# Windowed attention beside a gMLP: one fixed order from attention through its output projection, seven exponential buffers, two maxima banks

## The chip, the cores and the metric

The kernel runs on one core of a Trainium2 chip. A core has five engines that work side by side and meet at semaphores: TensorE (PE, matmuls into PSUM, with its weight loads shown apart as PEld), VectorE (DVE), ScalarE (ACT), GpSimd (POOL) and SyncE (SP), which here issues all DMA transfers. Every engine takes its instructions in the order in which they stand in its own queue. The metric is the device time of one execution in microseconds, taken as the median of several runs.

## What is computed

```python
def _A_ref(x, wqkv, wo):                      # H = 32 heads of 18, window 256
    q, k, v = ...                             # x @ wqkv
    scores = einsum("bhqd,bhkd->bhqk", q, k) * (Dh ** -0.5)
    mask = (q_idx - k_idx >= 0) & (q_idx - k_idx < W)
    p = softmax(where(mask, scores, -1e9))
    return (p @ v) @ wo

def _B_ref(x, w_in, w_sp, b_sp, w_out):       # S = 2048, D = 576, Fh = 2304
    z = gelu(x @ w_in)
    z1, z2 = z[..., :Fh], layernorm(z[..., Fh:])
    g = einsum("ts,bsf->btf", w_sp, z2) + b_sp[None, :, None]
    return (z1 * g) @ w_out

xn = layernorm(x)
out = x + _A_ref(xn, wqkv, wo) * silu(_B_ref(xn, w_in, w_sp, b_sp, w_out))
```

## The kernel before

All large products run in a 32-bit format on TensorE that keeps only the upper part of a number, so each operand is split into a high part (an ACT copy) and a low part (a subtraction on DVE or POOL), and three products are added: high by high, high by low, low by high. The stages follow each other: layer norm and the projections to q, k, v and z2 (up to about 425 us of the trace); then **the attention, with the z1 projection as filler**; then **the output projection of the attention** (its matmuls are named wops); then the spatial product with w_sp (acc, from about 945 us) and the last product with w_out.

The attention works in 16 units of four heads and 1024 queries (`UNITS`, `NU`). The q and k of a unit are read from DRAM into slots (tiles `att`, line 550). For each unit:

- *Maxima* (`max_item`, tile `sp`): a matmul of 128 queries with up to 384 keys, then on DVE an addition of the band mask (`band`) with the row maximum (line 606). When all 32 of a unit are done, `max_split` puts the negative maxima into the tile `ms`, two transposes on TensorE and two DVE copies bring them into `mhl` (`max_turn`), and a DMA moves them as two extra rows beside q (line 637), so that the next matmul subtracts them.
- *Scores* (`scores`, tile `tps`, line 741): a matmul over a block of 128 keys, the exponential on ACT into the tile `pt` (line 745), masking of the two edge blocks on POOL (lines 753 and 756). One `pt` tile holds four heads of one key block.
- *Value products* (`pv`, tile `ops`, line 769): four heads in four column groups of TensorE; the column of ones in the values gives the sum of the exponentials. A step takes one `pt` tile: four matmuls.
- *End of a unit* (`finish`): the sums go through DRAM (`den`, `r_d`) and come back, inverted, as a broadcast tile `rp` (line 814); POOL multiplies (line 818, four divisions to a unit) and SP stores the result to `o_d` (line 823).

Maxima, scores and the matmuls of z1 use 64 of TensorE's 128 rows each: heads of even number and the bank `ma` the upper half, heads of odd number and `mb` the lower half, so two of them run at a time. Value products and wops use all rows.

The z1 projection (`z1_rows`, line 685) has 18 chunks of 128 features; for each half of the rows and each of two spans of 512 tokens, 27 matmuls (`STEPS`) add up in one bank. The weights of a chunk come by DMA into `z1raw`, and are split by ACT into `z1wh` and by POOL into `z1wl` (line 702). A finished bank is copied by ACT to `z1o` (line 690) and stored (line 573).

**What sets the order.** Within a region opened by `tc.manual_schedule` the instructions of the named engines stay in the order in which the code emits them. In the attention the code picks that order itself: a loop keeps an estimated clock for each half of the rows (`row_time`) and for ACT, DVE and POOL (`busy`), and at each step emits, on the half that is free first: a run of value products if `pv_now` allows it, else a transpose of maxima, else a score or a maximum that its estimate says can go, else one filler matmul of z1. A score needs a free score bank (`done_exp`), a free `pt` buffer (`PTB` of them) and moved maxima; a maximum needs a free bank among `SPB` (`done_max`). A run of value products starts when enough `pt` tiles are ready: nine blocks of 128 queries, or all `PTB` tiles in use. Transfers are put into the same order by estimated due times (`after`). Score and maxima banks share five banks of PSUM (`5 - SPB` and `SPB`).

Attention and projection stand in two such regions, one behind the other, and instructions of the second may be placed among the last of the first.

In the projection, `wo_split` rounds the attention output of 256 tokens (tile `ohl`: ACT line 1175, DVE line 1176, from a load at lines 999 and 1001), and `wo_half` multiplies 128 tokens with wo (line 1189, 28 matmuls); there are 16 of these half tiles. The ninth is the first that needs the result of the last unit.

## Time and profile before

| | us |
|---|---|
| three runs | 1841.81, 1843.65, 1845.96 |
| median | 1843.65 |
| the profiled execution, whole | 1847.18 |
| its span in the trace | 1845.3 |
| busy in the span: PE / PEld | 1822.1 / 1597.3 |
| busy in the span: DVE / ACT / POOL | 1133.8 / 945.1 / 430.4 |
| first score matmul (tps) starts | 442.18 |
| first matmul of the spatial product (acc) starts | 944.65 |

The profile lists busy time by engine, groups of instructions by line with the mean duration of one and the idle time ahead of them (and who ended it), waits, and a timeline. A matmul's duration is its way through the array, and several are under way at a time; what one costs is read from the distance between starts. "Granted clock" (PEclk) is TensorE's clock as a share of full speed. In a row of the timeline, x8 means eight records of that kind in succession.

### The profile page before, as it was taken

The numbers are of one execution on the slowest core, as the hardware profiler recorded it, in microseconds if no ns is written. First come the engines' busy times: TensorE is split into PE (matmuls) and PEld (weight loads), VectorE is DVE, ScalarE is ACT, GpSimd is POOL, SyncE is SP. The second block draws the span as 40 slices with busy tenths as digits, with TensorE's granted clock in tenths as the row PEclk, the third lists the DMA queues.
The fourth block names the chain that finished last, engine by engine and source line by source line (L and its number), as shares of the span: only waits on it lengthen the run. The fifth ranks groups of instructions, "written<-read, shape, count | busy, mean of one in ns | idle before, by whom it ended". The sixth has DMA issues, their size and how long they took to land.

```text
span 1845.3 us, 37698 instructions
## 1 busy us (share of the span) xinstructions
PE 1822.1 (99%) x14373; PEld 1597.3 (87%) x14373; DVE 1133.8 (61%) x2299; ACT 945.1 (51%) x1757; POOL 430.4 (23%) x509
## 2 busy tenths in 40 slices
PE   8999999999999999999999999999999999999998
PEld 8999999998778777877888888888888888899998
DVE  7321333468777776631156788667886576767876
ACT  5433322225777667774467566465554544544443
POOL 3332333435566456554000000111100000000000
PEclk9999999999999999999999999999999999999999
DMA  8895688888677867645776777789776556796554
GB/s 275 189 234 166 233 279 280 289 265 234 160 194 189 206 176 199 179 140 150 224 244 223 242 239 247 256 291 302 253 256 235 189 188 208 229 269 208 160 162 135
DMA packets 266916, 405.72 MB, mean 220 GB/s; under 512 B 52336, under 2 KB 180592, under 8 KB 266608
## 3 DMA queue, kind: packets, MB, share of 16 engines
q1 hardware_dynamic: 266736, 403.32, 72.0%
q8 instruction: 113, 1.85, 0.4%
q14 instruction: 67, 0.55, 0.1%
HBM read 285.35 MB, written 117.09 MB: 218 GB/s over the span
## 4 chain that ended last, share of the span: by engine, by line
PE 85%; DMA 5%; DVE 5%; ACT 2%; SPq 1%; issue 1%; POOL 0%; DVEq 0%; ACTq 0%; POOLq 0%
PE acc L1470 34%; PE mb L207 11%; PE c L1562 8%; PE ma L685 6%; PE mb L685 6%; PE ma L207 5%; PE ops L769 4%; PE tps L741 3%; PE wops L1189 3%; PE sp L603 3%; DMA st_d<-qkhl 1%; SPq L364 1%; PE mb L381 1%; DMA att<-st_d 1%; DVE spl L117 1%
## 5 line engine op out<-in xcount | busy, mean ns | idle before, releaser
L1470 PE MATMUL acc<-spl,zh 128*128 128x512 f32 x1008 | 392.6, 389 | 0.9 <-DVE spl L117 0.6
L1470 PE MATMUL acc<-sph,zh 128*128 128x512 f32 x1008 | 392.3, 389 | 1.1 <-ACT so L1222 1.1
L1470 PE MATMUL acc<-sph,zl 128*128 128x512 f32 x1008 | 392.2, 389 | 0.0
L606 DVE CUSTOM_DVE_ANT_0 sp<-sp,band 128x384 f32<-128x384 f32 (+1 forms) x512 | 265.0, 566 | 77.4 <-PE sp L603 43.4
L745 ACT ACTIVATE pt<-tps 128x384 f32<-128x384 f32 (+2 forms) x576 | 229.0, 441 | 99.6 <-PE tps L741 74.9
L117 DVE TENSOR_TENSOR spl<-spr,sph 128x1024 fp32r<-128x1024 f32 x168 | 210.2, 1251 | 43.8 <-ACT sph L116 42.8
L685 PE MATMUL mb<-b,z1wh 64*128 64x512 f32 x648 | 225.6, 399 | 0.1
L1470 PEld LDWEIGHTS acc<-spl,zh 128*128 128x128 f32 x1008 | 189.2, 188 | 41.8 <-DVE spl L117 2.6
L1470 PEld LDWEIGHTS acc<-sph,zh 128*128 128x128 f32 x1008 | 189.2, 188 | 40.8 <-ACT so L1222 1.5
L685 PE MATMUL ma<-b,z1wh 64*128 64x512 f32 x648 | 222.8, 401 | 0.4 <-ACT zt L968 0.4
L1470 PEld LDWEIGHTS acc<-sph,zl 128*128 128x128 f32 x1008 | 189.2, 188 | 39.1
L116 ACT ACTIVATE zh<-b 128x384 fp32r<-128x384 f32 x168 | 87.4, 520 | 208.1 <-PE acc L1470 208.0
L116 ACT ACTIVATE sph<-spr 128x1024 fp32r<-128x1024 f32 x168 | 176.0, 1047 | 17.6 <-DMA spr<-in_w_sp_dram 9.2
L117 DVE TENSOR_TENSOR zl<-b,zh 128x384 fp32r<-128x384 f32 x168 | 98.5, 586 | 123.2 <-ACT zh L116 117.8
L741 PE MATMUL tps<-att 56*128 56x384 f32 (+1 forms) x576 | 171.7, 343 | 2.4 <-DMA att<-mhl 1.8
L603 PE MATMUL sp<-att 54*128 54x384 f32 (+1 forms) x512 | 159.5, 349 | 1.3 <-DMA att<-st_d 0.9
L1562 PE MATMUL c<-b,o 128*128 128x288 f32 x1056 | 143.8, 295 | 1.9 <-DVE o L117 1.4
L1562 PEld LDWEIGHTS c<-b,o 128*128 128x128 f32 x1056 | 141.0, 188 | 2.6 <-DVE o L117 1.9
L969 DVE BATCH_NORM_STATS2 st<-zt 128x6 f32<-128x384 f32 x96 | 49.3, 549 | 131.5 <-ACT zt L968 131.3
L685 PE MATMUL ma<-b,z1wl 64*128 64x512 f32 x324 | 128.5, 397 | 0.0
L685 PE MATMUL mb<-b,z1wl 64*128 64x512 f32 x324 | 127.9, 395 | 0.0
L685 PEld LDWEIGHTS mb<-b,z1wh 64*128 64x128 f32 x648 | 117.9, 186 | 6.4 <-ACT z1o L690 1.5
(224 smaller groups left out, 4203.0 us busy)
## 6 DMA issues: line engine op xcount, KB each, us to landing
spr<-sc_d SPq DMA_DIRECT2D x96, 512.0 KB
spr<-in_w_sp_dram SPq DMA_DIRECT2D x72, 512.0 KB
zr<-z_d SPq DMA_DIRECT2D x144, 192.0 KB
z_d<-zt SPq DMA_DIRECT2D x48, 384.0 KB
z_d<-z1o SPq DMA_DIRECT2D x72, 256.0 KB
z1t<-z_d SPq DMA_DIRECT2D x72, 256.0 KB
y_d<-z1t SPq DMA_DIRECT2D x72, 256.0 KB
a<-in_w_sp_dram SPq DMA_DIRECT2D x64, 256.0 KB
```

Source lines behind the costliest of these rows:

```text
L116: act.activation(hi, src, AF.Copy)
L117: dve.tensor_tensor(lo, src, f32(hi), ALU.subtract)
L207: pe.matmul(banks[h][:, :n], *both[h][i], start=i == 0, stop=i == STEPS - 1)
L603: pe.matmul(ps[:, :w], q_of(u, j)[0:54, i * P:(i + 1) * P], k_of(u, j)[0:54, k0:k0 + w], start=True, stop=True)
L606: dve.tensor_tensor_reduce(out=ps[:, :w], in0=ps[:, :w], in1=band[:, m0:m0 + w], scale=1.0, scalar=-3.0e38, op0=ALU.add, op1=ALU.max, accu ...
L685: pe.matmul(ps, w, x_, start=n == 0, stop=n == STEPS - 1)
L741: pe.matmul(ps[:, :m * P], k_of(u, j)[:, (kb - base) * P:(kb - base + 1) * P], q_of(u, j)[:, (a - lo) * P:(a - lo + m) * P], start=True, s ...
L745: act.activation(pt[:, j, d0:d0 + n * P], ps[:, (qa - a) * P:(qa - a + n) * P], AF.Exp, scale=scale)
L769: pe.matmul(o_ps[c][32 * j:32 * j + 32, (qa - 4 * c) * P:(hi - 4 * c + 1) * P], vgs[u][:, kb - k0, j * VW:j * VW + 32], pt[:, j, (qa - kb) ...
L1189: pe.matmul(po[:, i, :288], lt[:, cs], r[:, i * 288:(i + 1) * 288], start=n == 0, stop=n == len(pl) - 1)
L1470: pe.matmul(acc[j], z[:, ps], w[:, cs], start=s == i == 0 and n in OPENS, stop=s == 7 and i == 2, skip_group_check=True)
L1562: pe.matmul(banks[key][:, :288], y, w, start=begin and k == n == 0, stop=close and k == 8 and n == 2, skip_group_check=True)
```

## The change

- Two banks for maxima in place of three (`SPB`), and so three for scores in place of two; seven `pt` buffers in place of five (`PTB`).
- Room for them: `z1raw` has one buffer in place of two and is loaded with its chunk (no load one chunk ahead, `fetch_z1` goes); `rp`, `mhl` and `ms` have one buffer in place of two; `band` is 384 wide in place of 512. The tile `rp` is taken only when its load is emitted, after the divisions of the unit before.
- The maxima of the first two query blocks are reduced over the columns that can count (128 and 256 in place of 256), and the estimate for DVE becomes 132 + w ns in place of 600 or 470.
- A run of value products waits for twelve blocks in place of nine (or all `pt` buffers).
- If a score and a maximum can both go on a half, the maximum goes first; before, the one whose engine had been done sooner.
- Attention and projection are one region of fixed order.

```diff
-SPB = 3
-PTB = 5
+SPB = 2
+PTB = 7
...
-    band = const.tile([P, 512], F32, name="band")
+    band = const.tile([P, 384], F32, name="band")
     pool.memset(band, 0.0)
-    pool.memset(band[:, 384:512], NEG)
...
-            halved = [aa.tile([P, P], F32R, name=f"ms{i}", bufs=1) for i in range(2)]
-            for ms in halved:
-                pool.memset(f32(ms), 0.0)
+            halved = aa.tile([P, P], F32R, name="ms", bufs=1)
+            pool.memset(f32(halved), 0.0)
...
-                dve.tensor_tensor_reduce(out=ps[:, :w], in0=ps[:, :w], in1=band[:, m0:m0 + w], scale=1.0,
+                w = 384 - m0
+                dve.tensor_tensor_reduce(out=ps[:, :w], in0=ps[:, :w], in1=band[:, m0:384], scale=1.0,
...
-                done_max.append(use("dve", 600 if w > 256 else 470))
+                done_max.append(use("dve", 132 + w))
...
-                    turned[u] = aa.tile([64, P], F32, name="mhl")
+                    turned[u] = aa.tile([64, P], F32, name="mhl", bufs=1)
...
-            def fetch_z1(f):
-                if f < FH // P and f not in z1raws:
-                    z1raws[f] = zw.tile([P, 9, P], F32, name="z1raw", bufs=2)
-                    sp.dma_start(z1raws[f], w_z1[f])
-
             def load_z1(f):
-                fetch_z1(f)
-                raw = z1raws[f]
-                wh = zw.tile([P, 9, P], F32R, name="z1wh")
-                wl = zw.tile([P, 9, P], F32R, name="z1wl")
+                raw = zw.tile([P, 9, P], F32, name="z1raw", bufs=1)
+                sp.dma_start(raw, w_z1[f])
+                wh, wl = (zw.tile([P, 9, P], F32R, name=n) for n in ("z1wh", "z1wl"))
...
-                                if b == 1 and n == 20:
-                                    fetch_z1(f + 2)
...
-                while len(parts.get(u - 2, ())) > 4:
-                    part(u - 2)
                 den = aa.tile([P, HS // 32], F32, name="den")
-                rp = ap_.tile([P, HS], F32, name="rp", bufs=2) if u < NU - 1 else f32(slots[4][:, 0:HS])
+                at = []
+
+                def rp():
+                    if not at:
+                        while len(parts.get(u - 1, ())) > 4 and u < NU - 1:
+                            part(u - 1)
+                        at.append(ap_.tile([P, HS], F32, name="rp", bufs=1) if u < NU - 1 else
+                                  f32(slots[4][:, 0:HS]))
+                    return at[0]
...
-                heads.enter_context(tc.manual_schedule(engines=ENGINES | {ET.Activation, ET.SP}))
+                order.enter_context(tc.manual_schedule(engines=ENGINES | {ET.Activation, ET.SP}))
...
-                        return n if size >= 9 or len(pts) >= PTB or not score_queue[0] else 0
+                        return n if size >= 12 or len(pts) >= PTB or not score_queue[0] else 0
...
-                        ready.append((done_exp[-1], 0))
+                        ready.append(0)
...
-                        ready.append((done_max[-1], 1))
+                        ready.append(1)
...
-                    if min(ready)[1]:
+                    if ready[-1]:
...
-            order.enter_context(tc.manual_schedule(engines=ENGINES | {ET.Activation, ET.SP}))
```

What this does to the order of instructions is seen in the queues. First TensorE in an early unit, around one run of value products; L603 and L741 are maxima and scores, L685 is z1, L769 the value products. Before:

```order
L685 MATMUL ma<-b_96,z1wh 128x512
L685 MATMUL mb<-b_97,z1wh 128x512
L769 MATMUL ops<-pt,vg 32x128 x4
L769 MATMUL ops<-pt,vg 32x256 x4
L769 MATMUL ops<-pt,vg 32x384 x4
L741 MATMUL tps<-att_6807 128x256
L603 MATMUL sp<-att_2213 128x384
```

and TensorE in the change, at a run near the same place (the lines are now L676, L758, L601 and L730):

```order
L676 MATMUL ma<-b_96,z1wh 128x512
L676 MATMUL mb<-b_92,z1wl 128x512
L758 MATMUL ops<-pt,vg 32x128 x4
L758 MATMUL ops<-pt,vg 32x256 x4
L758 MATMUL ops<-pt,vg 32x384 x8
L758 MATMUL ops<-pt,vg 32x256 x4
L758 MATMUL ops<-pt,vg 32x128 x4
L601 MATMUL sp<-att_2214 128x384 x2
L730 MATMUL tps<-att_2212 128x384 x2
```

The run holds six steps where it held three, and two maxima follow it ahead of the scores. Over the whole attention there were 68 runs (47 of three steps, 11 of one, 8 of two, 2 of four) and there are now 44 (14 of six, 2 of five, 12 of four, 5 of three, 8 of two, 3 of one).

Next TensorE at the seam between z1 (L685, now L676) and the projection (L1189, now L1183). Before, the first wops of all stand here, with z1 behind them again:

```order
L685 MATMUL mb<-b_96,z1wh 128x512
L1189 MATMUL wops<-att_2215,ohl_14367 128x288 x2
L1189 MATMUL wops<-att_6807,ohl_14367 128x288 x2
L1189 MATMUL wops<-att_2215,ohl_14367 128x288 x4
L1189 MATMUL wops<-att_6807,ohl_14367 128x288 x2
L1189 MATMUL wops<-att_2215,ohl_14367 128x288 x4
L1189 MATMUL wops<-att_6807,ohl_14367 128x288 x2
L685 MATMUL ma<-b_92,z1wh 128x512
```

and in the change, TensorE's last matmuls of z1 with the first wops behind them:

```order
L676 MATMUL mb<-b_93,z1wh 128x512
L676 MATMUL mb<-b_96,z1wh 128x512
L676 MATMUL mb<-b_93,z1wl 128x512
L1183 MATMUL wops<-att_2214,ohl_14361 128x288 x2
L1183 MATMUL wops<-att_6802,ohl_14361 128x288 x2
L1183 MATMUL wops<-att_2214,ohl_14361 128x288 x4
```

Before, 56 wops stood in four bursts among the last z1 matmuls; now none does.

Last, SP's queue of transfers at the same seam: z1 stores (L573 and L1153, now L572 and L1148), loads of attention output for the projection (L999 and L1001, now L994 and L996), the last unit's sums (den) and z2 for the spatial product (zr). Before:

```order
L830 DMA den<-att_13723 128x1x32
L150 DMA zr<-z_d 128x384 x4
L573 DMA z_d<-z1o 128x2x256
L828 DMA r_d<-den 128x32
L999 DMA att_13723<-o_d 128x4x256
L1001 DMA att_13723<-o_d 64x256 x2
L150 DMA zr<-z_d 128x384 x2
L573 DMA z_d<-z1o 128x2x256 x5
L999 DMA att_2213<-o_d 128x4x256
L1001 DMA att_2213<-o_d 64x256 x2
```

and SP in the change, where z1raw (L646) is the load of the last chunk of z1's weights:

```order
L572 DMA z_d<-z1o 128x2x256 x3
L646 DMA z1raw<-in_w_z_dram 128x1152
L572 DMA z_d<-z1o 128x2x256 x7
L994 DMA att_2212<-o_d 128x4x256
L996 DMA att_2212<-o_d 64x256 x2
L994 DMA att_2213<-o_d 128x4x256
L996 DMA att_2213<-o_d 64x256 x2
L1148 DMA z_d<-z1o 128x2x256 x2
L826 DMA den<-att_13613 128x1x32
L149 DMA zr<-z_d 128x384 x4
L824 DMA r_d<-den 128x32
```

The last unit's sums and the first loads of z2 stood among the z1 stores and now stand behind all of them; the load of the second 256 tokens stood behind the fifth of five stores, with one more store to come, and now has two stores behind it.

10 lines of the change are left out of this document (4 added, 6 removed).

## The prediction

> **What bounds the kernel now.** I read the busy time by stretch first, because the page's shares are averages over stages with different limits.
>
> ```profile
> core 0: us, PE busy (x) PEld busy (x) DVE busy (x) ACT busy (x) POOL busy (x), PEclk, DMA share, GB/s
> 431.00:857.00 426.00, 422.30 (x4260) 330.58 (x4256) 282.55 (x1044) 294.15 (x732) 240.21 (x352) 1.00 0.71 182
> 857.00:887.00 30.00, 29.68 (x198) 24.13 (x197) 0.90 (x3) 3.12 (x6) 0.00 (x0) 1.00 0.37 115
> 887.00:945.00 58.00, 54.63 (x394) 54.31 (x395) 15.24 (x19) 30.40 (x43) 2.54 (x2) 0.94 0.74 242
> ```
>
> The change acts on the first two stretches (attention with the z1 projection as filler, then the rest of that filler) and on where the third begins. In the first, TensorE is busy 422.3 of 426.0 us; DVE 282.6, ACT 294.2 and POOL 240.2 have room. So almost no waiting is left to remove here, and a shorter order of TensorE's own work is what can pay. Who TensorE waited for, between 430 and 890 us, says the same:
>
> ```profile
> engine line waited for: us in total, times, longest us
> PE tps L741 <- DMA att<-mhl: 1.8, 1, 1.8
> PE sp L603 <- DMA att<-st_d: 0.9, 1, 0.9
> ```
>
> The filler ends with the largest gap of the region, seen in TensorE's timeline:
>
> ```profile
> 886.39 0.39 PE L685 MATMUL ma<-b,z1wl 64*128 64x512 f32 x1
> 890.37 6.92 PE L1189 MATMUL wops<-att,ohl 128*128 128x288 f32 x33 [3.59 <-ACT ohl L1175]
> ```
>
> 3.59 us idle, until ACT has rounded the next 256 tokens of the attention output. That came late because SP stood in its queue behind five stores of z1:
>
> ```profile
> 862.23 21.81 SPq L573 DMA_DIRECT2D z_d<-z1o  x5
> 884.13 0.42 SPq L999 DMA_DIRECT2D att<-o_d  x1
> ```
>
> **Term 1: fewer switches into the value products.** A busy TensorE is not an efficient one. Maxima, scores and z1 use half the rows each and run in pairs; the value products (ops) use all rows, so before and behind each run of them both halves must drain and refill. TensorE's timeline at the end of the attention prices it:
>
> ```profile
> 846.65 0.39 PE L685 MATMUL mb<-b,z1wh 64*128 64x512 f32 x1
> 846.65 0.39 PE L685 MATMUL ma<-b,z1wl 64*128 64x512 f32 x1
> 846.97 1.50 PE L769 MATMUL ops<-pt,vg 128*32 128x128 f32 x24
> 848.41 0.49 PE L685 MATMUL ma<-b,z1wh 64*128 64x512 f32 x1
> 848.74 0.40 PE L685 MATMUL ma<-b,z1wh 64*128 64x512 f32 x1
> ...
> 852.04 0.50 PE L685 MATMUL ma<-b,z1wl 64*128 64x512 f32 x1
> 852.47 0.43 PE L769 MATMUL ops<-pt,vg 128*32 128x128 f32 x8
> 852.82 0.50 PE L685 MATMUL ma<-b,z1wh 64*128 64x512 f32 x1
> 853.16 0.40 PE L685 MATMUL ma<-b,z1wh 64*128 64x512 f32 x1
> 853.40 0.39 PE L685 MATMUL ma<-b,z1wl 64*128 64x512 f32 x1
> 853.63 0.40 PE L685 MATMUL ma<-b,z1wh 64*128 64x512 f32 x1
> ```
>
> Undisturbed, pairs start every 0.233 us (853.16, 853.40, 853.63). A matmul of ops leaves two records, and four heads make one step, so x8 is one step (here one block of 128 queries) and x24 three steps (1 + 2 + 3 = 6 blocks, by the shapes in the order). The short run: from 852.04 to 853.16 pass 1.12 us, less two pair steps of 0.233, leaves 0.65 us for one block. The long run: 846.65 to 848.74 is 2.09, less 0.47, leaves 1.62 us for six. So a block costs (1.62 - 0.65) / 5 = 0.19 us and a run, before its first block, 0.65 - 0.19 = 0.46 us. Both runs have 512-column z1 pairs beside them; many others have scores or maxima of 384 columns, whose half drains sooner, so I take 0.40 us. The order of before has 68 runs (47 of them of three steps), that of the change 44 (14 of six, 12 of four). 24 x 0.40 = **9.6 us saved**; ends: 0.30 each (7.2) and 0.46 each (11.0). The number of blocks, of maxima, of scores and of z1 matmuls is the same in both orders.
>
> **Term 2: the projection no longer starts inside z1.** Before, 56 wops matmuls stand in four bursts among the last z1 pairs; now all 448 follow the last z1 matmul. Their own time only moves. The four bursts go, each a drain and refill like a run of ops: 4 x 0.40 = **1.6 us saved**, ends 0 and 3, as each burst also left one half to run alone for some steps, which may or may not come back elsewhere.
>
> **Term 3: the gap at the seam.** The first wops now waits for the last z1 matmul, then for ACT: the last copy of z1 stands ahead of the rounding in ACT's order, and a DVE subtraction follows.
>
> ```profile
> 883.06 0.60 ACT L690 ACTIVATE z1o<-mb 128x512 f32<-128x512 f32 x1 [2.89 <-PE mb L685]
> 889.04 1.27 ACT L1175 ACTIVATE ohl<-att 128x1280 fp32r<-128x1280 f32 x1 [1.58 <-DMA att<-o_d]
> 855.58 1.55 DVE L1176 TENSOR_TENSOR ohl<-att,ohl 128x1024 fp32r<-128x1024 f32 x1 [10.95 <-ACT ohl L1175]
> ```
>
> 0.60 + 1.27 = 1.9 us until the first four products, which need the high part alone; then about 0.7 more until the low part: those four take about 0.5 of the subtraction's 1.2 to 1.55. About 2.6 us in place of 3.59, so **1.0 us saved**; ends 0 and 3.6. The load of the next tokens (L999) now stands ahead of the last two z1 stores, about 6 us before they can go (27 pair steps of 0.233), so that wait goes. What becomes late next is the last unit's denominator, whose chain (den, r_d, rp, division, store) now begins behind the seam; its use is in the ninth of 16 half tiles, 8 x 28 matmuls of 0.139 us or 31 us later, so I cost that at nothing; without that cover it would be another gap like the 3.6 us here.
>
> A gap has a second price here, TensorE's clock:
>
> ```profile
> 886.00:888.00 2.00, 0.78 (x4) 0.29 (x2) 0.00 (x0) 0.60 (x1) 0.00 (x0) 1.00 0.93 260
> 890.00:892.00 2.00, 1.64 (x5) 1.36 (x6) 1.62 (x2) 2.00 (x5) 0.00 (x0) 0.50 0.54 191
> 892.00:894.00 2.00, 2.00 (x10) 2.00 (x10) 0.85 (x2) 1.91 (x3) 0.00 (x0) 0.50 1.01 279
> 894.00:896.00 2.00, 2.00 (x13) 2.00 (x13) 1.38 (x3) 0.35 (x1) 0.00 (x0) 0.73 0.92 240
> ...
> 626.00:628.00 2.00, 1.12 (x10) 1.00 0.59 221
> 628.00:630.00 2.00, 1.11 (x6) 0.71 0.45 119
> 630.00:632.00 2.00, 2.00 (x14) 0.50 0.68 222
> ```
>
> After the seam the granted clock is 0.50 for some 4 us: 0.8 + 1.0 + 0.5 = 2.3 us lost. (The last three rows show TensorE alone.) A wait of 1.8 us at 627 halved it as well, so 2.6 us will, and I keep the 2.3 us in the time. [...]
>
> **What the change takes in return.** It pays with buffers, each of which can turn into a wait in an engine that works in order.
>
> ```profile
> L606 DVE CUSTOM_DVE_ANT_0 sp<-sp,band 128x384 f32<-128x384 f32 (+1 forms) x477 | 247.8, 568 | 76.1 <-PE sp L603 42.5 <-PE tps L741 26.6 <-PE mb L685 2.1
> L606 DVE DVE_READ_ACCUMULATOR2_ANT mx<- 128x1 f32 x477 | 67.4, 141 | 0.0
> L603 PE MATMUL sp<-att 54*128 54x384 f32 (+1 forms) x477 | 148.1, 350 | 1.2 <-DMA att<-st_d 0.9 <-DMA z_d<-z1o 0.3
> L818 POOL TENSOR_TENSOR ou<-ou,rp 128x256 f32<-128x256 f32 x60 | 43.8, 746 | 7.0 <-DMA o_d<-ou 3.4 <-DMA att<-st_d 2.0 <-DMA rp<-r_d 1.7
> ...
> 408.90 6.26 DMA z1raw<-in_w_z_dram
> ```
>
> - Two banks for maxima, three for scores. One pass through a bank takes 0.350 (matmul) + 0.568 (DVE) + 0.141 (read of the maximum) = 1.06 us, so two banks carry one maximum each 0.53 us; the stretch has 426 / 477 = 0.89 us for each. On average that holds; in bursts TensorE waits, and with it the scores and z1 queued behind on both halves. The 32 maxima whose width falls from 256 to 128 spare DVE 0.13 us each by the code's own 132 + w, hidden since DVE has 143 us free. I take 1 us lost, ends -1 (scores wait less with three banks) and +20 (worked out below).
> - One z1raw buffer: the load is now issued at the first z1 step of a chunk, its first use by ACT 29 steps later. 29 x 0.233 = 6.8 us at least, against 6.26 for the one such load that the chain shows. Queued behind a late ACT copy are the exponentials, then TensorE. I take 0.5; ends 0 and 4 (four late places of 1 us).
> - One rp buffer: SP's load of the next inverses waits for POOL's four divisions of the unit before, 4 x 0.746 = 3 us, with the q and k loads and the z1 stores behind it in SP's queue. In one unit of the order the load follows right behind these divisions; in the others more work lies between. I take 0.5; ends 0 and 3.
> - One ms and one mhl buffer: the 5 us allowed for a move lies between their uses; nothing, at most 1.
>
> Sum: -9.6 - 1.6 - 1.0 + 2.0 = **-10.2 us**. The profiled execution took 1847.18 us around a span of 1845.3, 3.5 us above the median of the runs shown; I expect 1837 of such an execution and **1833.5** for the median 1843.65. The stalls at 627 and 669 us (1.8 and 0.9 us idle, with 1.11 x 0.29 + 2.00 x 0.50 = 1.3 of half clock after the first) I leave standing, for their loads stay.
>
> **Rivals.** *The stalls in the region go too* (maxima now go ahead of scores, so their moves are earlier): 4.0 less, 1829.5. For it: both waits are for loads of a unit about to begin. Against: the loads start when they did. Chance 0.08. *The clock stays full after the seam*, its gap being 1 us shorter than now: 2.3 less, 1831. Against it stands the row at 627; chance 0.05. [...] *The saving is eaten* by rp and z1raw, whose upper ends are 7 us, or by a den chain that comes late for the ninth half tile (3.6): between 1840 and 1847, around 1843. For it: SP and ACT work in order and have one buffer less to run ahead with. Chance 0.17. *Slower: two banks too few.* The order is laid out as if a bank were free 0.516 us after DVE begins (132 + 384 ns in the code) plus 0.15 of guard; the rows give 0.568 + 0.141 = 0.709, short by 0.043 us. If most of the 480 maxima stood at that limit, TensorE would wait 480 x 0.043 = 20.6 us: 1843.65 - 10.2 + 20.6 = 1854. It decides from 10.2 / 480 = 0.021 us each. Against: 0.89 us per maximum on average, and each wait delays the maxima behind it as well, so waits don't repeat in every item. Chance 0.13. *The change doesn't do what it says*: the order shows runs of six steps, so seven buffers are used; no chance of its own.
>
> **How the numbers follow.** The forecast alone (1828 to 1840) has 0.57; with the two rivals below it 0.70 for faster by over 0.2% (3.7 us, about what a measurement of this kernel can tell from no change), 0.17 within, 0.13 slower. The range leaves out most of the slower case and the far end of the gains: 1826 (term 1 and 2 at 11 and 3, stalls gone) to 1846.
>
> **What would show it.** Right: 44 runs of ops; the first tps to the last z1 matmul shorter by 7.8 us of moved wops (56 of the 394 that took 54.63 us) and about 10 more; one gap of 2 to 3 us ahead of wops, ended by ACT ohl, with the clock at 0.50 after it. Wrong: TensorE waiting for DVE at sp by more than the few us of now (two banks), ACT z1wh waiting for z1raw, SP's rp waiting for POOL, or a gap inside the wops for ohl. If the region shrinks but the seam grows by as much, term 3 has failed.

## The result, and the profile after

| | before | after |
|---|---|---|
| median, us | 1845.96 (1841.81 to 1846.89) | 1860.53 (1853.01 to 1862.90) |
| span of the profiled execution | 1845.3 | 1860.8 |
| first score matmul (tps) starts | 442.18 | 448.21 |
| last z1 matmul ends | 886.78 | 895.47 |
| first matmul of the spatial product (acc) | 944.65 | 959.48 |

The ratio is 1.0075, 95% interval 1.0059 to 1.0091: the change is slower by 0.75%, outside the forecast range. The first lines of the profile's page after the change (span; busy time of each engine) show TensorE busy for 5 us longer and idle for 10 us longer (33.7 us in place of 23.2). The two profiled executions differ by 15.5 us, the medians by 14.6:

```profile
span 1860.8 us, 37645 instructions
PE 1827.1 (98%) x14373; PEld 1587.4 (85%) x14373; DVE 1142.1 (61%) x2299; ACT 934.1 (50%) x1757; POOL 432.5 (23%) x507
```

**A loss before the attention.** I follow the program from the front. Busy time by stretch (length; busy time of PE, PEld, DVE, ACT, POOL with the number of instructions; granted clock; DMA) in the last part of the z2 stage, before:

```profile
380.00:425.00 45.00, 44.85 (x499) 43.07 (x495) 29.78 (x96) 8.23 (x20) 18.59 (x16) 1.00 0.88 282
425.00:431.00 6.00, 5.59 (x44) 4.67 (x45) 5.93 (x13) 3.74 (x5) 5.92 (x6) 1.00 0.78 278
```

and after:

```profile
380.00:425.00 45.00, 41.92 (x470) 40.65 (x468) 27.16 (x86) 7.61 (x19) 16.31 (x13) 1.00 0.88 275
425.00:431.00 6.00, 4.68 (x46) 3.85 (x44) 4.71 (x14) 1.82 (x6) 5.51 (x5) 1.00 0.00 1
```

TensorE idles for some 3 us more up to 425 us. The timeline of TensorE after the change shows one of the places (in brackets the idle time ahead and who ended it):

```profile
399.79 0.34 PE L206 MATMUL mb<-z2w,b 64*128 64x384 f32 x1
400.68 0.38 PE L601 MATMUL sp<-att 54*128 54x256 f32 x1 [0.56 <-DVE mx L605]
```

and that of DVE what it did meanwhile:

```profile
398.70 0.56 DVE L965 BATCH_NORM_STATS2 st<-zt 128x6 f32<-128x384 f32 x1 [3.00 <-ACT zt L964]
399.29 0.32 DVE L970 BATCH_NORM_AGGREGATE mv<-st 128x2 f32<-128x36 f32 x1
399.52 0.50 DVE L965 BATCH_NORM_STATS2 st<-zt 128x6 f32<-128x384 f32 x1
400.06 0.32 DVE L970 BATCH_NORM_AGGREGATE mv<-st 128x2 f32<-128x36 f32 x1
400.30 0.27 DVE L605 CUSTOM_DVE_ANT_0 sp<-sp,band 128x128 f32<-128x128 f32 x1
```

The maxima of unit 0 are laid into the z2 matmuls at fixed steps (line 954). DVE is held by the statistics of z2, which wait for ACT's gelu; two maxima fill both banks, and the third matmul waits, with every z2 matmul behind it. The list of waits from 380 to 431 us has four such places, 3.0 us together, ahead of TensorE's matmuls, and none before the change; a fifth gap of 0.8 us ahead of a maximum has no cause in the list. With three banks the third maximum had a bank. The last matmul of z2 ends at 430.06 us in place of 425.12, so 4.9 of the 6.0 us by which the first tps is late arise here, and the rest behind it.

**The attention.** From the first tps to the last z1 matmul, before and after:

```profile
442.18:886.78 444.60, 441.13 (x4367) 345.35 (x4364) 273.91 (x1009) 293.92 (x730) 236.68 (x348) 1.00 0.69 177
```

```profile
448.21:895.47 447.26, 438.40 (x4313) 337.86 (x4311) 280.67 (x1006) 283.07 (x729) 237.28 (x348) 0.98 0.66 173
```

The first holds 7.8 us of wops that the second doesn't, so what is left takes 447.3 us in place of 436.8. Idle: 8.9 in place of 3.5. The clock stands at 0.50 in three stretches after the change, and in one before (628.80 to 632.20 us, with 3.31 us busy):

```profile
449.10:452.50 3.40, 3.40 (x21) 3.32 (x21) 1.83 (x8) 2.18 (x6) 0.98 (x2) 0.50 0.68 177
623.10:629.90 6.80, 6.09 (x28) 5.65 (x30) 2.82 (x9) 4.22 (x10) 1.76 (x3) 0.50 0.69 201
688.00:691.40 3.40, 3.40 (x20) 3.28 (x19) 2.50 (x9) 1.54 (x4) 1.90 (x4) 0.50 0.70 151
```

After the change, z1 matmuls on one half start 0.43 us apart at 0.50 (`ma` at 624.93, 625.36 and 625.78 us) and 0.23 us apart at 1.00 (616.22, 616.46 and 616.69 us), so I count half of that busy time as lost to the clock, an estimate: 6.5 us after, 1.7 before. What is left, busy time as at full clock, is 441.1 - 7.8 - 1.7 = 431.6 before and 438.4 - 6.5 = 431.9 after. The forecast had it fall by 11.

Why it didn't fall shows in the view of the maxima's tile `sp`, which lists why engines sat idle before the tile's instructions (us, times). Before:

```profile
  DVE mx L606: 4.0, 9
```

After:

```profile
  DVE mx L605: 20.6, 64
```

TensorE waited 64 times, 0.32 us each, nearly always at the weight load (PEld) of a maximum. I read it so, and no view shows it directly: the half of the rows whose weight load waits stands still, while the other may run on alone, and TensorE counts as busy while it does half the work.

The longest wait, in the timeline of all engines but PEld:

```profile
620.94 0.61 SPq L830 DMA_DIRECT2D den<-ou  x1
...
621.17 0.34 PE L601 MATMUL sp<-att 54*128 54x384 f32 x1
...
622.26 1.59 SPq L549 DMA_DIRECT2D att<-st_d  x3
623.81 1.22 PE L730 MATMUL tps<-att 56*128 56x384 f32 x3 [2.30 <-DMA att<-mhl]
```

A score waited 2.3 us for moved maxima, and the granted clock is 0.50 from 623.1 us on.

**The seam** went as forecast. Timeline of TensorE, then the stretch up to the first acc:

```profile
895.08 0.39 PE L676 MATMUL mb<-b,z1wl 64*128 64x512 f32 x1
897.36 1.33 PE L1183 MATMUL wops<-att,ohl 128*128 128x288 f32 x4 [1.89 <-ACT ohl L1169]
```

```profile
895.47:959.48 64.01, 62.12 (x449) 61.84 (x449) 18.70 (x21) 32.45 (x45) 3.45 (x2) 0.95 0.73 239
```

One gap of 1.89 us, ended by ACT's rounding, and no other: the late chain of the last unit costs nothing. Before, the stretch took 57.9 us and 7.8 of its work lay in the region ahead: 65.7. So 1.7 us are gained.

The spans differ by 15.5 us: 6.0 up to the first tps, +0.3 of busy time at full clock, +5.4 idle, +4.8 half clock, -1.7 at the seam, +0.7 behind the first acc.

### The profile page after: what moved, and what is told of

The parts are those of the page before. It is cut to its first block, busy times and chain, and to the rows that moved or that the text cites. A ratio compares the mean times of both kernels' runs of the same rounds, so it can differ in the third digit from the quotient of the medians.

```text
span 1860.8 us, 37645 instructions
## 1 busy us (share of the span) xinstructions
PE 1827.1 (98%) x14373; PEld 1587.4 (85%) x14373; DVE 1142.1 (61%) x2299; ACT 934.1 (50%) x1757; POOL 432.5 (23%) x507
## 4 chain that ended last, share of the span: by engine, by line
PE 81%; DMA 6%; DVE 6%; SPq 3%; ACT 2%; issue 2%; POOL 0%; DVEq 0%; ACTq 0%; POOLq 0%
PE acc L1464 32%; PE mb L206 11%; PE c L1556 8%; PE ma L676 6%; PE ma L206 5%; PE mb L676 5%; PE ops L758 4%; PE wops L1183 3%; PE sp L601 3%; PE tps L730 2%; SPq L363 1%; DVE sp L605 1%; DMA st_d<-qkhl 1%; DMA att<-st_d 1%; DVE spl L116 1%
## 5 line engine op out<-in xcount | busy, mean ns | idle before, releaser
L605 DVE CUSTOM_DVE_ANT_0 sp<-sp,band 128x384 f32<-128x384 f32 (+2 forms) x512 | 268.8, 547 | 92.5 <-PE sp L601 80.0
L734 ACT ACTIVATE pt<-tps 128x384 f32<-128x384 f32 (+2 forms) x576 | 215.9, 454 | 51.6 <-PE tps L730 37.7
L676 PE MATMUL ma<-b,z1wh 64*128 64x512 f32 x648 | 225.8, 403 | 0.6 <-ACT zt L964 0.6
L676 PE MATMUL mb<-b,z1wh 64*128 64x512 f32 x648 | 225.9, 402 | 0.4 <-ACT z1o L681 0.4
L601 PE MATMUL sp<-att 54*128 54x384 f32 (+1 forms) x512 | 178.6, 379 | 9.8 <-DVE mx L605 5.1
L730 PE MATMUL tps<-att 56*128 56x384 f32 (+1 forms) x576 | 161.2, 335 | 3.0 <-DMA att<-mhl 2.3
L601 PEld LDWEIGHTS sp<-att 54*128 54x128 f32 x512 | 90.1, 187 | 47.3 <-DVE mx L605 20.6
L676 PE MATMUL ma<-b,z1wl 64*128 64x512 f32 x324 | 130.2, 402 | 0.0
L676 PE MATMUL mb<-b,z1wl 64*128 64x512 f32 x324 | 129.0, 398 | 0.0
```

The source lines that it names most:

```text
L601: pe.matmul(ps[:, :w], q_of(u, j)[0:54, i * P:(i + 1) * P], k_of(u, j)[0:54, k0:k0 + w], start=True, stop=True)
L605: dve.tensor_tensor_reduce(out=ps[:, :w], in0=ps[:, :w], in1=band[:, m0:384], scale=1.0, scalar=-3.0e38, op0=ALU.add, op1=ALU.max, accum_o ...
L676: pe.matmul(ps, w, x_, start=n == 0, stop=n == STEPS - 1)
L730: pe.matmul(ps[:, :m * P], k_of(u, j)[:, (kb - base) * P:(kb - base + 1) * P], q_of(u, j)[:, (a - lo) * P:(a - lo + m) * P], start=True, s ...
L734: act.activation(pt[:, j, d0:d0 + n * P], ps[:, (qa - a) * P:(qa - a + n) * P], AF.Exp, scale=scale)
```

## The experiments

A row of this table is made as above, from the region between the first tps and the last z1 matmul (the wops that stand in it taken out: 7.8 us for 56 matmuls in the kernel before, 5.8 us for 42 in `before_two_maxima_banks`). "Ratio" is against the kernel before, measured beside each; the waits for DVE (us) are those at `sp` between 431 and 857 us.

```
run                            ratio [95%]             runs of  waits for  idle  half   busy at
                                                        ops     DVE mx           clock  full clock
before                         1                         68       4.0      3.5   1.7    431.6
after                          1.0075 [1.0059, 1.0091]   44      20.6      8.9   6.5    431.9
three_maxima_banks             1.0097 [1.0068, 1.0126]   54       8.5     16.3   9.1    429.1
before_two_maxima_banks        1.0061 [1.0041, 1.0081]   76       9.8     12.0   4.9    435.1
later_bank_estimate            1.0105 [1.0074, 1.0136]   (value products left behind the last z1)
z2_maxima_spread               1.0042 [1.0029, 1.0056]   44      17.6      8.4   1.7    433.1
old_buffers_new_rules          1.0004 [0.9994, 1.0014]   72      11.3      2.7   0.0    434.5
single_buffers_old_rules       1.0003 [0.9992, 1.0014]   65       1.8      8.1   5.1    426.4
spread_two_raw_six_pt          1.0094 [1.0070, 1.0117]   65      16.0     10.3   3.9    436.3
spread_two_rp_six_pt           1.0053 [1.0032, 1.0075]   65      16.7      6.5   3.4    436.0
spread_old_buffers             1.0157 [1.0139, 1.0175]   75      23.7     17.2  11.2    437.2
spread_old_rules               1.0126 [1.0105, 1.0148]   62       8.5     19.3   9.9    433.1
spread_old_cost                0.9975 [0.9964, 0.9986]   43       8.9      5.6   1.7    426.1
three_banks_old_rules_two_raw  0.9981 [0.9968, 0.9993]   65       3.2      4.7   0.0    427.6
old_cost_alone                 1.0009 [0.9998, 1.0019]   43      10.0      9.6   4.8    427.0
spread_old_cost_old_priority   1.0010 [0.9997, 1.0023]   45       9.7     12.3   5.8    424.3
spread_ten_ns_more             1.0065 [1.0044, 1.0085]   47      20.1     11.3   6.8    430.5
spread_measured_cost           1.0258 [1.0226, 1.0290]   (value products left behind the last z1)
spread_600_472_344             1.0025 [1.0006, 1.0043]   46       9.3     11.0   4.6    426.5
spread_old_cost_from_nine      1.0101 [1.0065, 1.0138]   61      10.0     16.1   7.8    432.8
```

### First batch: banks, bank times and the z2 stage

`three_maxima_banks`, the change with the old number of banks:

```diff
-SPB = 2
+SPB = 3
```

> The change with one number put back: three banks for maxima and two for scores; seven pt buffers, single buffers, priority and the new DVE estimate stay. Theory A (two banks are too few, both in the z2 stage, where maxima stand at fixed places, and in the attention): the first score matmul starts at about 442 us again (448.2 in the change), TensorE's weight loads for sp wait for DVE under 5 us (20.6 in the change), and the time falls to 1833-1840. Theory B (the single buffers of z1raw and rp make SP, ACT and POOL wait): the first 6 us come back, the rest stays, 1853-1856. Theory C (maxima ahead of scores make bursts that TensorE waits for): as B, 1850-1856.

The z2 stage is as before (first tps at 442.2), and waits for DVE fall to 8.5 us. But the attention is 7 us longer than in the change, which none of the three theories had. Other waits took over, in the list of waits from the first tps to the last z1:

```profile
POOL ou L814 <- DMA rp<-r_d: 14.3, 5, 5.7
POOL ou L814 <- DMA att<-st_d: 12.0, 2, 8.0
...
PE ops L758 <- POOL pt L742: 6.4, 2, 5.2
PE tps L730 <- ACT pt L734: 5.8, 4, 2.5
```

Divisions of a finished unit wait in POOL's queue for the load of the one `rp` tile; the masks stand behind them, and TensorE's value products wait for masks. The two banks alone don't explain the loss.

`before_two_maxima_banks`, the kernel before with one bank less:

```diff
-SPB = 3
+SPB = 2
```

> The kernel before with two banks for maxima and three for scores, nothing else. Theory A: the z2 stage loses its 6 us (first score matmul at 448), the attention little, as its estimate for DVE there is 600 or 470 ns and so later than the bank is free: 1850-1856. Theories B and C: single buffers and priority are as before, so 1844-1848, but for what the z2 stage shows.

Slower by 0.61%: the banks hurt without any of the other edits. Four gaps of the z2 stage are there (3.3 us together). Idle time and half clock in the attention grow by 12 us and the work by 3.5; Theory A had little loss there.

`later_bank_estimate`, the change with a bank taken as free 200 ns later, DVE's own time unchanged:

```diff
-                done_max.append(use("dve", 132 + w))
+                done_max.append(use("dve", 132 + w, 200))
```

> The change, with a maxima bank taken as free 200 ns later than now (332 + w in place of 132 + w, for the bank alone; the estimate of DVE's own time stays). The first score matmul stays at 448. Theory A: the waits of TensorE's weight loads for DVE at sp fall from 20.6 to under 8 us and the time to 1845-1852. Theories B and C: the time stays within 3 us of 1860, since buffers and priority are the same.

Waits for DVE fell to 6.7 us, but the time did not. In the view of `z1wh`, the reasons why ACT sat idle before it begin with

```profile
  DMA z1raw<-in_w_z_dram: 24.0, 6
```

(3.7 us in the change), and the z1 filler ran out 18 us before the last value product. It counts against "DVE waits explain it all".

`z2_maxima_spread`, the change with the maxima of unit 0 over more of the z2 stage, behind the steps that clash with the statistics:

```diff
-                            if pc == 5 and q > 2 and n % 4 == 1 and ahead:
+                            if pc == 5 and q > 1 and n % 4 == 1 and n > 8 and ahead:
```

> The change, with the 30 of 32 maxima that are laid among the last z2 products put at steps 9, 13, 17, 21 and 25 of six 128-token pieces in place of steps 1, 5, ... 25 of five, so that they come after DVE's batch statistics of the piece before; the last two follow behind. Theory A for the z2 stage: the six gaps of about 1.1 us ahead of sp go, the first score matmul starts at 442-444, and the whole gets 4-6 us shorter, 1854-1856. If those gaps are only moved (a wait for a load comes in their place), the time stays at 1860.

The ratio falls by 0.33 points, 6.1 us, and the first tps comes at 443.0 in place of 448.2, though two waits for DVE, 1.7 us together, are left in the stage. The z2 stage's part of the loss is thereby shown; the runs named spread_ keep this edit.

### Second batch: the buffers or the rules

"Rules" are the edits to the loop that picks the order: maxima first, a maximum costed at 132 + w, value products from 12 blocks. `old_buffers_new_rules` is the change with `SPB` 3, `PTB` 5 and two each of `rp`, `z1raw` (with its early load) and `mhl`:

```diff
-SPB = 2
-PTB = 7
+SPB = 3
+PTB = 5
...
-                    turned[u] = aa.tile([64, P], F32, name="mhl", bufs=1)
+                    turned[u] = aa.tile([64, P], F32, name="mhl")
...
+            def fetch_z1(f):
+                if f < FH // P and f not in z1raws:
+                    z1raws[f] = zw.tile([P, 9, P], F32, name="z1raw", bufs=2)
+                    sp.dma_start(z1raws[f], w_z1[f])
...
-                        at.append(ap_.tile([P, HS], F32, name="rp", bufs=1) if u < NU - 1 else
+                        at.append(ap_.tile([P, HS], F32, name="rp", bufs=2) if u < NU - 1 else
```

> The change with every buffer of the kernel before (three banks for maxima, five exponential buffers, two inverse tiles, two z1 raw tiles with the old early load, two mhl), but with the change's rules: maxima ahead of scores, maxima costed at 132 + w, runs of value products of 12 blocks or full, one region, the narrower band. Theory A (the single tiles and the banks cause the loss in the attention, the rules are harmless or good): the waits of ACT z1wh for z1raw and of POOL ou for rp fall from 7.6 and 14.1 us (three banks, single tiles) to under 2 us each, and the time is that of the kernel before less the 1 to 2 us that the later projection spares: 1840 to 1847. Theory B (the rules cause it: work leaves in an order whose stalls are there whatever the buffers): the waits of TensorE at tps and sp stay, and the time is 1852 to 1862.

1.0004: the rules alone do no harm, as Theory A had it. This has the least idle time of all (2.7 us) and no half clock, but short runs and 434.5 us of work. `single_buffers_old_rules` is the reverse, with three banks:

```diff
-SPB = 2
+SPB = 3
...
-                done_max.append(use("dve", 132 + w))
+                done_max.append(use("dve", 600 if w > 256 else 470))
...
-                        return n if size >= 12 or len(pts) >= PTB or not score_queue[0] else 0
+                        return n if size >= 9 or len(pts) >= PTB or not score_queue[0] else 0
...
-                        ready.append(0)
+                        ready.append((done_exp[-1], 0))
...
-                        ready.append(1)
+                        ready.append((done_max[-1], 1))
...
-                    if ready[-1]:
+                    if min(ready)[1]:
```

> The change's single tiles and seven exponential buffers, three banks for maxima, but the old rules: a maximum or a score by which was free first, the old costs of 600 and 470 ns, runs of value products from 9 blocks. Theory A (the single z1 raw and inverse tiles cause the loss): ACT z1wh waits for z1raw and POOL ou for rp as in the change with three banks (7.6 and 14.1 us in all), and the time is 1855 to 1864. Theory B (the rules cause it): the stalls of TensorE of over 1.8 us in the attention go from six or more to two or three as before, and the time is 1838 to 1847, whatever ACT and POOL wait for.

1.0003, as Theory B had it: the single tiles cost nothing on balance. They are not free, for idle time and half clock are 8.0 us above the kernel before, but the work is 5.2 us below it. So the first run speaks for one theory and the second for the other, and neither tiles nor rules by themselves make the 1862 us of three banks with single tiles *and* new rules.

`spread_two_raw_six_pt` and `spread_two_rp_six_pt` give `z2_maxima_spread` one of its tiles back (the lines of `z1raw` or of `rp` just shown), for six `pt` buffers:

```diff
-PTB = 7
+PTB = 6
```

> The change with the maxima of unit 0 spread over the z2 stage (1853.8 measured), and two z1 raw tiles with the old early load; their room is paid by six exponential buffers in place of seven. Theory A1 (the single z1 raw tile is the larger cost: its load lands late, ACT waits and the exponentials stand behind it): ACT z1wh waits for z1raw under 1 us, the half-clock stretches that begin behind such waits go, and the time is 1845 to 1849. Theory A2 (the single inverse tile, or the banks): within 2 us of 1853.8, or above, as runs of value products get shorter (up to 2 us).

> The change with the maxima of unit 0 spread over the z2 stage (1853.8 measured), and two inverse tiles; six exponential buffers in place of seven. Theory A2 (the single inverse tile is the larger cost: SP's loads wait for the divisions, POOL waits for rp, and band masks and q and k loads stand behind): POOL ou waits for rp under 3 us (18 us with one), and the time is 1845 to 1849. Theory A1 (the z1 raw tile, or the banks): within 2 us of 1853.8 or above.

Neither gained (1.0094 and 1.0053 against 1.0042): with 65 runs of ops in place of 44 both had 3 us more of work, and most of the DVE waits stayed. Neither tile is shown to be the cause by itself; as a `pt` buffer was given up for it, these runs don't test a tile alone.

### Third batch: two banks with old buffers, old rules, old cost

`spread_old_buffers` is `z2_maxima_spread` with the buffers of before, banks aside (the diff of `old_buffers_new_rules` without `SPB`); `spread_old_rules` is it with the three old rules (the diff of `single_buffers_old_rules` without `SPB`); `spread_old_cost` has only the first of them:

> The change with two maxima banks and its new rules, the maxima of unit 0 spread over the z2 stage, and the old buffers (five exponential buffers, two inverse tiles, two z1 raw tiles with the early load, two mhl). With one tile each and seven exponential buffers it took 1853.8; with three banks and old buffers the new rules took 1844.9. Theory S (single tiles are what the attention pays for): 1843 to 1847. Theory B (two banks are): 1851 to 1857, with DVE as TensorE's releaser at sp for over 12 us in all.

> The change with two maxima banks, single tiles and seven exponential buffers, the maxima of unit 0 spread over the z2 stage, and the old rules (by which bank was free first, 600 and 470 ns for a maximum, value products from 9 blocks). Theory R (the rules turn the scarce buffers into stalls, as with three banks, where the old rules took 1845.5 and the new ones 1862.3): 1843 to 1847. Theory B (two banks cost the rest whatever the rules): 1850 to 1856.

```diff
-                done_max.append(use("dve", 132 + w))
+                done_max.append(use("dve", 600 if w > 256 else 470))
```

> Only two edits on the change: the maxima of unit 0 spread over the z2 stage, and a maximum laid out at the old 600 and 470 ns of DVE in place of 132 + w (516, 388 or 260); the trace has 0.709 us for a wide one. Theory C (of the rules it is the cost that is too low: DVE is behind its plan, so whatever is placed by the plan's time waits): DVE's waits at sp fall from 20 us to under 8, no stall of TensorE over 2 us, 1840 to 1846. Theory P (priority or run length): within 2 us of the 1853.8 without this edit.

The first two are 29 and 23 us slower than before, and neither theory had that. In `spread_old_buffers` one wait took 7.7 us, as TensorE's timeline shows:

```profile
696.67 0.39 PE L683 MATMUL ma<-b,z1wh 64*128 64x512 f32 x1
704.77 0.65 PE L601 MATMUL sp<-att 54*128 54x384 f32 x1 [7.71 <-DMA att<-st_d]
```

It waited for a load of q and k. The third is **faster than before by 0.25%**. Its region, and the waits at `sp`:

```profile
441.17:874.55 433.38, 427.75 (x4316) 339.58 (x4312) 288.75 (x1010) 280.50 (x730) 237.20 (x348) 1.00 0.68 179
```

```profile
  DVE mx L605: 8.9, 22
```

The waits for DVE halved (to 8.9 us, where under 8 was expected), the work at full clock fell by 7 us against `z2_maxima_spread`, and idle time by 2.8.

`three_banks_old_rules_two_raw` is `single_buffers_old_rules` with two `z1raw` tiles, loaded early as before, and six `pt`:

```diff
-PTB = 7
+PTB = 6
...
-                raw = zw.tile([P, 9, P], F32, name="z1raw", bufs=1)
-                sp.dma_start(raw, w_z1[f])
+                fetch_z1(f)
+                raw = z1raws[f]
```

> A candidate that may beat both: the run with three banks, single tiles and old rules (1845.5) lost 7 us in three stalls behind single tiles; here two z1 raw tiles with the early load come back, for six exponential buffers in place of seven. If the stalls behind z1raw go and no others come: 1839 to 1843. If six buffers shorten the runs of value products by as much, or the inverse tile's stalls take over: 1844 to 1848.

0.9981: the second version that beats the kernel before. Idle and half clock fell from 13.2 to 4.7 us; so in this order, with three banks and the old rules, it does pay to give this tile back.

### Last batches: the cost by itself, and luck

`old_cost_alone` is the change with the cost edit just shown and nothing else:

> One edit on the change: a maximum laid out at the old 600 and 470 ns in place of 132 + w. Theory C (the cost is what the attention pays for, and the fixed places of unit 0 in the z2 stage the rest, the two adding up): 20 us less 6.7 us for the places, so 13 less than the change: 1846 to 1849, with six waits of some 1.1 us for DVE between 399 and 430 us as in the change, and 5 us or less of waits for DVE at sp behind them. Rival (the two edits only work together, as the order behind the places is another): 1852 to 1861.

The time is as Theory C had it: 1.0009, 12 us less than the change (1847.6 us). Its waits are not: 10.0 us for DVE at `sp` where 5 or less were expected, and four places ahead of them in place of six. The first tps is late (445.2), and spreading the maxima as well is worth another 0.34 points, as it was on the change. The two edits add up.

`spread_old_cost_old_priority` and `spread_old_cost_from_nine` each give the fastest version one old rule back (the lines of `ready`, and that of `size`, in the diff of `single_buffers_old_rules`):

> The fastest so far (spread maxima in z2, old cost; 1840.5) with the old choice between a maximum and a score, by which bank was free first. The same with value products from 9 blocks as well took 1869.9. Theory P (the choice is what lost those 29 us: with three score banks the scores win, maxima come late and the masks with them): 1860 to 1872. Theory T (it is the run length): 1840 to 1846.

> The fastest version (1840.5) with value products from 9 blocks or full buffers, as before, in place of 12. With the old choice between maximum and score alone it took 1846.9, with both 1869.9. If runs of 12 blocks are what seven buffers are for (43 runs, against some 60 from 9 blocks, 17 more at 0.16 to 0.4 us): 1843 to 1848. If the run length accounts for most of the 23 us between: 1855 to 1865.

The choice costs 6 us, the run length 23: the theory that it is the choice fell. From nine blocks, the work grows by 6.7 us, runs rise from 43 to 61 and, in this order, idle time and half clock from 7.3 to 23.9 us.

`spread_ten_ns_more` and `spread_600_472_344` ask how much is luck; against `z2_maxima_spread` each changes one number (the second 216 in place of the 142):

```diff
-                done_max.append(use("dve", 132 + w))
+                done_max.append(use("dve", 142 + w))
```

> A control for how much of any such difference is luck of the order: the change with spread maxima (1853.8), a maximum laid out at 142 + w in place of 132 + w, 10 ns more. If the time follows the cost smoothly (13 us for 84 ns at the wide maxima): 1851 to 1854. If another order with nearly the same cost can fall out quite differently: outside 1848 to 1858.

> A second control for the luck of the order, beside the fastest version (1840.5): spread maxima, and a maximum laid out at 216 + w, which is the old 600 ns for the wide ones, 472 in place of 470 for the middle ones, and 344 in place of 470 for the narrow ones (some 30 of 512). If what counts is that a bank's 600 + 150 ns covers the 709 that the trace shows for a wide maximum: DVE waits at sp of 6 to 11 us and 1837 to 1845. If the 1840.5 was a lucky order: 1846 to 1856.

Ten nanoseconds moved the ratio by 0.23 points, 4 us, though the two intervals still overlap. 216 + w is the old cost for all but the narrow maxima, yet its ratio is 0.5 points above that of `spread_old_cost`, clear of both intervals. So the fastest version owes part of its gain to a lucky order, as the second theory had it. The region of `spread_600_472_344`:

```profile
442.38:884.52 442.14, 431.11 (x4309) 340.90 (x4307) 288.95 (x1004) 280.79 (x728) 237.91 (x348) 0.99 0.65 173
```

The busy time at full clock agrees with that of `spread_old_cost` to 0.4 us (426.5 and 426.1), and so do the waits for DVE (9.3 and 8.9). The difference is all in idle time and half clock (15.6 against 7.3), behind other waits, of which its list shows

```profile
POOL ou L814 <- DMA rp<-r_d: 24.2, 6, 9.6
ACT z1wh L691 <- DMA z1raw<-in_w_z_dram: 9.2, 4, 4.1
...
PE tps L730 <- DMA att<-mhl: 4.8, 4, 2.8
```

`spread_measured_cost` lays a maximum out at 325 + w, the 709 ns that I took from the trace as the time of a wide one, 0.568 + 0.141 us. That sum is too long, for the two instructions of a maximum overlap. DVE's timeline after the change:

```profile
619.75 0.57 DVE L605 CUSTOM_DVE_ANT_0 sp<-sp,band 128x384 f32<-128x384 f32 x1
620.23 0.14 DVE L605 DVE_READ_ACCUMULATOR2_ANT mx<- 128x1 f32 x1
620.23 0.60 DVE L605 CUSTOM_DVE_ANT_0 sp<-sp,band 128x384 f32<-128x384 f32 x1
620.75 0.14 DVE L605 DVE_READ_ACCUMULATOR2_ANT mx<- 128x1 f32 x1
```

From the start of a maximum to the end of its read pass 0.62 and 0.66 us here, and the next maximum begins after 0.48. The expectation was:

> The change with spread maxima, a maximum laid out at what the trace shows: 325 + w, 709 ns for a wide one. Theory C alone (the closer to the measured time, the fewer waits): waits for DVE at sp under 3 us and 1836 to 1841. Rival (the order of this kernel is 109 ns x 480 = 52 us longer on DVE's side, the z1 filler runs out before the attention ends, and its last scores and value products stand without anything beside them): few waits for DVE, but 1850 to 1870.

The rival was right, and worse than put. The filler ends at 868.7 us, and value products, masks and copies then take turns alone, at a clock of 0.63 (the stretches before and after that moment):

```profile
442.15:868.70 426.55, 408.61 (x3950) 332.25 (x3949) 274.73 (x954) 246.40 (x632) 205.15 (x301) 0.98 0.63 168
868.70:933.74 65.04, 59.38 (x366) 32.05 (x365) 20.02 (x59) 36.51 (x98) 31.42 (x48) 0.63 0.34 94
```

### What the table gives together

A straight line through 18 rows (all but the two with value products behind z1) makes the busy time at full clock 412.3 us, plus 0.24 us for each run of ops (standard error 0.04), plus 0.43 us for each us of waiting for DVE at `sp` (0.07); the scatter about it is 1.8 us. The rows differ in other ways too, so these are averages over orders. Idle time and half clock are not in the line, and orders with nearly the same cost differ in them (above).

## Why the prediction was wrong

**The step that failed first** is in what bounds the kernel: "The change acts on the first two stretches." It acts on the z2 stage as well, where unit 0's maxima use the same banks at fixed places and DVE has other work. Price 6 us by the ratios, shown by `z2_maxima_spread` (first tps 5.2 us earlier) and again between `old_cost_alone` and `spread_old_cost` (4.0 us earlier).

**Term 1, fewer switches: right mechanism, taken too high.** The 44 runs came as said. A run of six steps takes 2.73 us to the next matmul,

```profile
468.39 2.80 PE L758 MATMUL ops<-pt,vg 128*32 128x128 f32 x48
471.12 0.44 PE L601 MATMUL sp<-att 54*128 54x384 f32 x2
```

where two runs of three take 2 x 1.44 (846.97 to 848.41 in the prediction's rows): 0.15 us saved there; what is saved ahead of a run these rows don't show. Over all rows a run costs 0.24, not 0.40, so 24 fewer save 5.8 us and not 9.6. Single pairs of runs spread about that: 18 more runs cost 6.7 us in `spread_old_cost_from_nine` (0.37 each), 21 more cost 3.2 and 2.9 us where a tile was given back (0.15 and 0.14). I had read the 0.46, from which I took 0.40, at two undisturbed places with 512-column neighbours.

**The two banks: named, priced as the slower rival, and taken at 1 us.** The rival had the right wait, TensorE for DVE at `sp`, which rose by 16.6 us, but not its sum. Its 0.043 us rest on the 0.709, and by the 0.62 to 0.66 us of the rows above a bank is free within the 0.666 that the order allows. It had 480 waits of 0.043 us; there were 64 of 0.32, and that both make 20.6 us is chance. The reason I gave against it held for the number of waits and not for their length. By the line's 0.43 the rise costs 7.1 us, more than the 5.8 that the longer runs saved. That the cost in the order brings most of these waits is shown, though not by which step of the plan: at 600 ns for a wide one they come to 8.9 to 10.0 us, at 516 and 526 to 17.6 to 20.6, with the same banks and tiles, and 43 to 47 runs.

**The single tiles: 0.5 + 0.5 us taken, with 7 as upper end.** Idle time and half clock rose by 10.2 us. Among the waits that grew are those for moved maxima, q and k loads, `rp` (POOL, 1.7 to 10.6 us) and `z1raw` (ACT, none to 3.7 us). No one tile could be shown to be the cause: giving one back did not help with two banks, and `z1raw` did help with three. With both banks and tiles scarce, six orders that differ by the z2 places and the cost alone (after, `z2_maxima_spread`, `old_cost_alone`, `spread_old_cost` and the two controls) lost between 7.3 and 18.1 us so. Where in that range an order lands can't be foretold from its rules here; that part stays open.

**Term 2** can't be told apart from the others in the busy time, and no run takes the one region of fixed order back. **Term 3 was right**: 1.7 us gained, a gap of 1.89 us ended by ACT, the half clock behind it kept (0.50 from 896.2 to 903.0 us), and the last unit's late denominator free. **The stalls at 627 and 669** did not go, as forecast; others joined them.

So most mechanisms were named, and beyond the z2 stage the sum failed on sizes: the gain from fewer runs was by the line 5.8 us of 9.6, the two banks cost 7.1 us and not 1, and the idle time and half clock that grew by 10.2 us stood against 1 us for the single tiles. Each wait was priced alone, though one of 2.3 us also came with 6.8 us of half clock.

## What to carry to other kernels

When a change takes a buffer away, look at every stage that uses it, also where its users stand at fixed places between other work. In an order laid out ahead by estimates, an engine time that is too short turns into waits of the engine that must not wait, and one that is too long uses up the filler: here 516 and 526 ns for a wide maximum lost, 709 lost most, and the orders that won had 600. An engine's time is read from start to end in its timeline, as the means of two instructions that overlap add up to too much (0.709 us where the timeline has 0.62 and 0.66). And before crediting a rule, change the estimate by a hair: 10 ns moved this kernel by some 4 us, about what its runs can tell apart, and 2 ns in the middle widths with 126 in the narrow ones by 9, so differences of that size between two orders say little about the rule.

## What the hardware showed

**Half clock behind a gap, and not behind every gap.** Inside the attention the granted clock is 0.50 from 449.1 to 452.5, from 623.1 to 629.9 and from 688.0 to 691.4 us after the change, in or behind idle times of TensorE of 1.38, 2.30 and 1.67 us; from 628.8 to 632.2 us before, at the end of one of 1.77 us; and from 699.8 to 713.5 us in `spread_old_buffers`, from within the 7.7 us wait on. A gap of that length does not always bring a stretch. At the seam, the rows of `old_buffers_new_rules` show

```profile
877.00:879.00 2.00, 1.98 (x9) 1.25 (x7) 0.00 (x0) 0.00 (x0) 0.00 (x0) 1.00 1.02 290
879.00:881.00 2.00, 0.13 (x1) 0.13 (x1) 0.15 (x1) 1.94 (x3) 0.00 (x0) 0.85 0.76 247
881.00:883.00 2.00, 2.00 (x7) 1.72 (x8) 1.94 (x4) 0.98 (x1) 0.00 (x0) 0.50 0.75 225
```

and those of `single_buffers_old_rules`

```profile
879.00:881.00 2.00, 2.00 (x18) 1.46 (x14) 0.00 (x0) 0.21 (x1) 0.00 (x0) 1.00 0.92 273
881.00:883.00 2.00, 0.18 (x1) 0.00 (x0) 0.00 (x0) 2.00 (x4) 0.00 (x0) 1.00 0.71 235
883.00:885.00 2.00, 1.45 (x9) 1.22 (x10) 1.87 (x3) 1.20 (x2) 0.00 (x0) 1.00 0.83 234
```

In the first three TensorE idles for 1.9 us and the clock falls to 0.50; in the second three it idles for 2.4 us and the clock stays at 1.00. No one figure divides all cases: after the change the clock fell at 896.2 us, 0.7 us into the gap at the seam, while 1.6 us idle (755.5 to 757.5 us, `three_banks_old_rules_two_raw`) left it at 1.00 up to 761.5 us. What decides stays open. So the prediction's rival "the clock stays full" could not be judged by the length of the gap alone. An idle time of 1.89 us, the seam after the change, came with a fall, and in `spread_old_cost` one of 1.13 us:

```profile
632.20 0.50 PE L676 MATMUL mb<-b,z1wh 64*128 64x512 f32 x1 [1.13 <-ACT z1o L681]
```

with the clock at 0.50 from 632.80 to 636.20 us.
